# Turning three more normalised chunks with VectorE instead of TensorE, and multiplying token tiles 5 to 8 in a row

## The chip, the cores and the metric

The kernel runs on one core of one Trainium2 chip. A core has five engines that matter here: TensorE (PE, matrix products), VectorE (DVE, elementwise work, reductions and transposes of 32 x 32 blocks), ScalarE (ACT, activations, that is a function of scale times input plus bias), GpSimd (POOL, slower elementwise work) and SyncE (SP, which issues the DMAs between DRAM and the on-chip memory). Each engine works through its own queue in order; semaphores make one engine wait for another. The metric is the time of one execution on the device in microseconds. All times below are microseconds unless marked otherwise.

## What is computed

One block of a transformer over 2048 tokens of width 512: an adaptive layer norm, linear attention with 32 heads, a second adaptive layer norm, and a bilinear feed-forward part.

```python
h = layernorm(x) * (1 + ca) + sa
q, k, v = split_heads(h @ wqkv)
pq, pk = phi(q), phi(k)                  # phi(t) = where(t > 0, t + 1, exp(t)) + 1e-6
kv = einsum("bhsd,bhse->bhde", pk, v);  z = pk.sum(over tokens)
o = (pq @ kv) / (pq . z + 1e-6)
x = x + ga * (o @ wo)
h = layernorm(x) * (1 + cb) + sb
x = x + gb * (((h @ w_gate) * (h @ w_up)) @ w_down)
```

The six vectors sa, ca, ga, sb, cb, gb come from `silu(c) @ w_mod`. Everything is in 32-bit floating point.

## The kernel before, in words

The tokens are cut into four chunks of 512 and each chunk into four token tiles of 128, 16 tiles in all, numbered 0 to 15; tiles 4 to 7 belong to the second chunk. (The change's title counts the tiles 4 to 7 as the fifth to the eighth.) A tile has its 128 tokens on the 128 partitions and 512 features along them. To keep 32-bit accuracy at the faster matmul format, every operand is split into a rounded part and a difference (`split`, L193: a copy with rounding on ScalarE, then a subtraction, mostly on VectorE), and every product is three matmuls: high by high, high by low, low by high (`product`, L207 to L209; 12 matmuls for a projection over four blocks of 128 features).

A projection needs the normalised tokens with features on the partitions, so each chunk is turned once per layer norm. Before the change, `Norm.transpose` (L289) does that for one block of 128 features with four TensorE transposes of 128 x 128 against an identity matrix (L293) into a PSUM bank; `Norm.modulated` (L302) then applies scale and shift on ScalarE and splits.

The order of the work is written out by hand: all queues run in the order of the program text. The pool `tiles` has 94 buffers of 128 x 512; a new tile takes a free buffer.

The main loop (L525) runs over the 16 tiles as steps i = 0 to 15, with i = 4 * chunk + j. In step i TensorE does the key projection of tile i + 2 (`proj`, L325), in steps 3, 4, 6 and 7 also a query projection (`q_at`), then `t_tile(i)` (L368), twelve matmuls that add keys times inputs to four accumulators. ScalarE and VectorE split tile i + 1's inputs and keys (`k_split_x`, `k_split`), apply phi to the projection (`k_phi`), and add up z. In steps j = 2 and 3 they take the statistics of the chunk after the next; in step j = 3 they normalise its first two tiles (`xhat`, L269), in the following step the other two. In the following steps j = 0 and j = 1 (`turn_at`) the chunk is turned, two blocks of features per step, between two halves of `t_tile`. The chunk turned in steps 4 and 5 is first wanted by the key projection in step 6, the one turned in steps 8 and 9 in step 10. `extra` hangs other work on single steps: splits of the value and output weights, parts of the six modulation vectors, loads.

After the loop come the attention's small product, the query tiles and the tail. There the query tiles of the later chunks are already turned by VectorE by a detour: `ready` (L744) divides by the denominator and stores a tile to DRAM with one DMA (`move_out`, L719), `move_in` (L725) reads it back with four DMAs in an order in which transposes of 32 x 32 blocks turn the whole tile, `turn_v` (L733) turns it, `turn_h` and `turn_l` split it. `y_step` (L777) multiplies a turned tile with the output weights (twelve matmuls, L766), starts the next tile's accumulator and takes the statistics of the last one for the second layer norm (`y_b`, L768, `stats_act`, L245). The third and fourth chunk's second norm is also turned by a detour (`stow`, `unstow`, `flip`, `flipped`): ScalarE normalises in an order of blocks (`xhat_blocks`, L275), VectorE turns tile by tile into one wide buffer, ScalarE makes from it one block of 128 features at a time. The first two chunks' second norm is turned by TensorE (`ln2_turn`, L914). `gate_up` (L842, 24 matmuls) and `down` (L865) are the feed-forward part for three of its eleven blocks of columns; the other eight are done by a fast matrix scheme for two chunks together (from L1030 in the profile).

SP issues all DMAs in the order of the program. A DMA that waits, for a free buffer or for data, holds up all those behind it.

## Time and profile before

| | us |
|---|---|
| median of three runs | 554.49 (553.96 to 555.14) |
| the profiled execution | 554.37 |
| span of its instructions | 552.7 |
| TensorE busy | 547.0 |
| VectorE busy | 373.6 |
| ScalarE busy | 291.7 |
| GpSimd busy | 203.4 |

The span runs from the first to the last instruction of the profiled execution; the rest of its time lies around it. Rows of groups give the line, engine, operation, output and input tiles, shapes and count, then the busy sum in microseconds and the mean of one in nanoseconds, then idle time of the engine just before them. Rows of a timeline give the start and the duration in microseconds from the span's start; neighbouring instructions of one line are merged with a count. Matmuls are pipelined: one of 128 x 512 is shown with about 390 ns but the next starts about 227 ns later, so TensorE's pace is read from starts.

### The profile page before, as it was taken

To read this page: it belongs to the slowest core of one execution; us is meant where nothing else is said; L and a number is where in the kernel's file an instruction comes from. 1 tells how busy PE (TensorE), PEld (TensorE's weight loads), DVE (VectorE), ACT (ScalarE), POOL (GpSimd) and SP (SyncE) were. 2 spreads that over 40 slices of the span, in tenths; PEclk is the share of its full clock that TensorE was granted. 3 is DMA by queue.
4 is the path that set the end of the run, shared out by engine and by line. 5 is a ranking of instruction groups with operands and counts; after the bars stand their busy time and mean duration, and the time that the engine had idled before them with its cause. 6 is when DMAs were issued, how large, how long until landed. Compare 5 with 4: busy or idle time off the path is not lost.

```text
span 552.7 us, 7324 instructions
## 1 busy us (share of the span) xinstructions
PE 547.0 (99%) x2488; PEld 449.2 (81%) x2488; DVE 373.6 (68%) x610; ACT 291.7 (53%) x539; POOL 203.4 (37%) x204
## 2 busy tenths in 40 slices
PE   8999999999999999999999999999999999999997
PEld 7788888888888878878888888877888888888886
DVE  7896968986887886778776576985444444434434
ACT  3695856646476667566684545454443444444110
POOL 2000000102003201057596666766666546446200
PEclk9999999999999999999999999999999999999999
DMA  8900203320503205845545071690434222200004
GB/s 284 387 15 2 76 20 103 108 77 1 157 2 133 96 5 186 267 145 135 160 111 155 0 230 38 216 322 2 133 116 132 59 57 59 58 20 0 1 0 152
DMA packets 58373, 58.28 MB, mean 105 GB/s; under 512 B 7328, under 2 KB 38304, under 8 KB 58336
## 3 DMA queue, kind: packets, MB, share of 16 engines
q1 hardware_dynamic: 58336, 57.83, 33.2%
q8 instruction: 19, 0.31, 0.2%
q14 instruction: 18, 0.15, 0.1%
HBM read 42.60 MB, written 15.20 MB: 105 GB/s over the span
## 4 chain that ended last, share of the span: by engine, by line
PE 99%; DVE 0%; issue 0%
PE bank L1030 33%; PE acc L766 7%; PE acc L1110 6%; PE acc L1111 6%; PE acc L1112 6%; PE bank L207 5%; PE bank L209 5%; PE bank L208 5%; PE acc L375 3%; PE acc L374 3%; PE acc L373 3%; PE bank L849 2%; PE bank L851 2%; PE bank L850 2%; PE acc L146 2%; PE bank L293 2%
## 5 line engine op out<-in xcount | busy, mean ns | idle before, releaser
L1030 PE MATMUL bank<-h,w 128*128 128x512 f32 (+1 forms) x798 | 184.7, 390 | 0.0
L1030 PEld LDWEIGHTS bank<-h,w 128*128 128x128 f32 (+1 forms) x798 | 148.4, 186 | 33.4 <-ACT bank L1035 0.7
L1035 ACT ACTIVATE bank<-bank 128x512 f32<-128x512 f32 (+1 forms) x38 | 22.2, 583 | 139.6 <-PE bank L1030 139.5
L836 DVE TENSOR_TENSOR x<-acc,x 128x512 f32<-128x512 f32 (+1 forms) x73 | 48.8, 682 | 48.4 <-PE acc L1112 47.7
L1016 POOL TENSOR_TENSOR w<-raw,w 128x256 fp32r<-128x256 f32 (+3 forms) x38 | 40.9, 1077 | 91.0 <-ACT w L1009 91.0
L1111 PE MATMUL acc<-w,kh 128*128 128x512 f32 (+2 forms) x154 | 59.6, 387 | 0.0
L1110 PE MATMUL acc<-w,kh 128*128 128x512 f32 (+2 forms) x154 | 59.6, 387 | 0.0
L1112 PE MATMUL acc<-w,kl 128*128 128x512 f32 (+2 forms) x154 | 59.5, 386 | 0.0
L263 POOL TENSOR_TENSOR rstd<-ve,half 128x4 f32<-128x4 f32 (+1 forms) x10 | 11.0, 1103 | 121.8 <-DVE ve L262 69.6
L195 POOL TENSOR_TENSOR w<-raw,w 128x512 fp32r<-128x512 f32 (+1 forms) x25 | 35.1, 1409 | 52.2 <-ACT w L194 47.3
L1016 POOL TENSOR_TENSOR w<-t,w 128x512 fp32r<-128x512 f32 (+1 forms) x38 | 49.2, 1318 | 0.0
L195 DVE TENSOR_TENSOR kl<-u,kh 128x512 fp32r<-128x512 f32 (+1 forms) x38 | 26.4, 736 | 30.6 <-ACT kh L194 30.6
L207 PE MATMUL bank<-w,h 128*128 128x512 f32 x104 | 40.9, 394 | 0.0
L209 PE MATMUL bank<-w,h 128*128 128x512 f32 x104 | 40.6, 391 | 0.0
L208 PE MATMUL bank<-w,h 128*128 128x512 f32 x104 | 40.6, 390 | 0.0
L766 PE MATMUL acc<-w,xh 128*128 128x512 f32 x120 | 37.4, 393 | 0.0
L1089 DVE TENSOR_TENSOR u<-bank,u 128x512 f32<-128x512 f32 (+1 forms) x19 | 13.1, 691 | 31.6 <-PE bank L1030 25.1
L1110 PEld LDWEIGHTS acc<-w,kh 128*128 128x128 f32 (+1 forms) x154 | 28.9, 188 | 6.0
L1112 PEld LDWEIGHTS acc<-w,kl 128*128 128x128 f32 (+1 forms) x154 | 28.9, 188 | 5.9
L1111 PEld LDWEIGHTS acc<-w,kh 128*128 128x128 f32 (+1 forms) x154 | 28.9, 188 | 5.9
L998 POOL TENSOR_TENSOR t<-raw,t 128x256 f32<-128x256 f32 (+1 forms) x34 | 25.9, 761 | 1.4
L766 PEld LDWEIGHTS acc<-w,xh 128*128 128x128 f32 x120 | 22.2, 188 | 4.6
(211 smaller groups left out, 1116.5 us busy)
## 6 DMA issues: line engine op xcount, KB each, us to landing
raw<-in_w_mod_dram SPq DMA_DIRECT2D x24, 256.0 KB, 3.7
raw<-in_B_w_down_dram SPq DMA_DIRECT2D x20, 256.0 KB, 3.2
raw<-in_B_w_gate_dram SPq DMA_DIRECT2D x36, 128.0 KB, 3.4
raw<-in_B_w_up_dram SPq DMA_DIRECT2D x36, 128.0 KB, 3.4
x<-in_A_x_dram SPq DMA_DIRECT2D x16, 256.0 KB, 5.4
out_dram<-x SPq DMA_DIRECT2D x15, 256.0 KB, 2.6
raw<-in_A_wqkv_dram SPq DMA_DIRECT2D x12, 256.0 KB, 5.4
moved<-h SPq DMA_DIRECT2D x12, 256.0 KB, 2.1
```

The lines of the kernel that those rows point to most:

```text
L195: (low or nc.vector).tensor_tensor(l, src, f32(h), op=ALU.subtract)
L207: nc.tensor.matmul(ps, ah, bh, start=i == 0, stop=False)
L208: nc.tensor.matmul(ps, ah, bl, start=False, stop=False)
L209: nc.tensor.matmul(ps, al, bh, start=False, stop=i == n - 1)
L766: nc.tensor.matmul(yps[i], x, y, start=False, stop=k == KD - 1 and x is al, skip_group_check=True)
L836: nc.vector.tensor_tensor(xt[:, a:b], dn[j][:, a:b], xt[:, a:b], op=ALU.add)
L998: sub = lambda out, x, y: (on or nc.gpsimd).tensor_tensor(out, x, y, op=ALU.subtract)
L1016: sub = lambda out, x, y: (on or nc.gpsimd).tensor_tensor(out, x, f32(y), op=ALU.subtract)
L1030: mm = lambda x, y, **kw: nc.tensor.matmul(ps, x[:, k], y, skip_group_check=True, **kw)
L1110: nc.tensor.matmul(ps, hh[:, a:b], dh[:n, c:d], start=i == 0, stop=False)
L1111: nc.tensor.matmul(ps, hh[:, a:b], dl[:n, c:d], start=False, stop=False)
L1112: nc.tensor.matmul(ps, hl[:, a:b], dh[:n, c:d], start=False, stop=i == len(hs) - 1)
```

## The change

Three chunks are no longer turned by TensorE: the first layer norm of the third and fourth chunks, and the second layer norm of the second chunk. Each takes the detour by DRAM instead: `xhat_blocks` for four tiles, one store per tile (`lift_out`), four loads per tile (`lift_in`), one VectorE transpose per tile into the wide buffer (`lift_turn`), then per block of 128 features one ScalarE pass with scale and shift (`lift_row`) and the split (`lift_parts`). All four tiles must be turned before the first block can be made. In the loop, all four tiles are normalised and stored at the end of step j = 3, loaded in the following j = 0, and turned and split in j = 1. In step 6 the query projection is put ahead of the key projection; the splits of the output weights move from steps 12 and 13 to 14 and 15. In the tail the query tiles 4 to 7 are multiplied one after the other, ahead of the third `gate_up` and of `down`; tiles 8 to 10 follow `down`; and the denominators, the moves of tiles 8 to 11 and the statistics are put in a new order around them. The first norm's own copies for the third and fourth chunks are now in block order, so `k_split_x` reads them with `by_row`.

```diff
+    LIFTED = (2, 3)
+    def lift_out(name, x):
+        to = tc.dram_tile([P, D], F32, name=name)
+        nc.sync.dma_start(to, x)
+        return to
+    def lift_in(of):
+        v = of.rearrange("(m i) (q c) -> q i m c", i=BL, c=P)
+        u = B("u")
+        for q in range(NQ):
+            nc.sync.dma_start(u[q * BL:(q + 1) * BL].rearrange("i (m c) -> i m c", c=P), v[q])
+        return u
+    def lift_turn(j, u):
+        nc.vector.transpose(wide[:, j].rearrange("p (m s i) -> p m s i", m=NQ, i=BL),
+                            u.rearrange("p (m s i) -> p m s i", m=NQ, i=BL))
+    def lift_row(k, scale, shift):
+        f = B("f")
+        nc.scalar.activation(f.rearrange("p (x i) -> p x i", i=BL),
+                             wide.rearrange("p j (m s i) -> p (j m) s i", m=NQ, i=BL)[:, :, k],
+                             AF.Identity, scale=scale[:, k:k + 1], bias=shift[:, k:k + 1])
+        return f
+    def lift_parts(k, f, cast=True):
+        h, l = B("h", dt=F32R), B("h", dt=F32R)
+        if k % 2 and cast:
+            nc.vector.tensor_copy(h, f)
+        else:
+            nc.scalar.activation(h, f, AF.Copy)
+        nc.vector.tensor_tensor(l, f, f32(h), op=ALU.subtract)
+        return h, l
...
-             12: lambda: (mod_part(4, 2, 3), wo_s.extend(split_raw(x) for x in raw_o[:2]), cols.update({3: col_out(3, mod_col(accs[3], bank()), 0.0)}), mod_load(5)),
...
+             14: lambda: (mod_part(5, 3), wo_s.extend(split_raw(x) for x in raw_o[:2])),
+             15: lambda: wo_s.extend(split_raw(x) for x in raw_o[2:])}
...
-    turn_at = {4 * ch + j: (ch + 1, 2 * j, 2 * j + 1) for ch in range(1, NCH - 1) for j in range(2)}
-    turn_at.update({1: (1, 0, 1), 2: (1, 2, 3)})
+    turn_at = {1: (1, 0, 1), 2: (1, 2, 3)}
...
+        up = ch + 1 if 0 < ch < NCH - 1 else None
+        if i == 6:
+            qps = proj(q_at[i], wq)
         if i > 2:
             ahead[i + 2] = proj(i + 2, wk) if i + 2 < NT else proj(i + 6 - NT, wq)
-        if i in q_at:
+        if i in q_at and i != 6:
             qps = proj(q_at[i], wq)
+        if up and j == 0:
+            lifts = [lift_in(x) for x in lifts]
+        if up and j == 1:
+            lift_turn(0, lifts[0])
...
             k_split(i + 1)
+        if up and j == 1:
+            lift_turn(1, lifts[1])
...
-            nx.xhat(0, 1)
+            nx.xhat_blocks(0, 1)
...
+        if ch + 2 < NCH and j == 3:
+            nx.xhat_blocks(2, 3)
+            lifts = [lift_out(f"first_{ch}_{n}", x) for n, x in enumerate(nx.n)]
...
         t_tile(i, *range(done, KD))
+        if up and j == 1:
+            lift_turn(2, lifts[2])
+            lift_turn(3, lifts[3])
+            for k in range(KD):
+                nx.t[k] = lift_parts(k, lift_row(k, ca, sa), cast=up == 2)
+            norm[up:] = [nx]
...
+    den_a(2, 0, 1, on=nc.vector)
     ln2_turn(0, 0, 1, cast=nc.vector)
...
-    den_a(2, 0, on=nc.vector)
+    turn_h(5)
+    turn_l(5)
+    y_seed(5)
     split_down(f1, nc.gpsimd)
     g()
-    y_step(4, lambda: scale_down(f2), lambda: den_a(2, 1, on=nc.vector))
+    y_step(4, lambda: turn_v(7), lambda: den_a(2, 2, on=nc.vector))
+    y_step(5, lambda: scale_down(f2))
+    y_step(6, lambda: den_a(2, 3, on=nc.vector))
+    y_step(7, turn=False, seed=False)
+    den_b(2)
     g = gate_up(0, f2)
...
+    ready(8, 9)
+    norm2[1].rstd_of(0, 3)
+    y_b(7)
+    ready(10)
+    norm2[1].nmr_of(0, 3)
+    norm2[1].rstd_of(3, 4)
+    norm2[1].xhat_blocks(0, 1, 2)
+    move_in(8, 9)
+    lifts = [lift_out(f"second_1_{n}", norm2[1].n[n]) for n in range(3)]
+    ready(11)
+    norm2[1].nmr_of(3, 4)
+    norm2[1].xhat_blocks(3)
+    lifts.append(lift_out("second_1_3", norm2[1].n[3]))
+    lifts[0], lifts[1] = lift_in(lifts[0]), lift_in(lifts[1])
+    move_in(10)
+    lifts[2], lifts[3] = lift_in(lifts[2]), lift_in(lifts[3])
+    move_in(11)
+    split_down(f2, nc.gpsimd)
     g()
...
+    turn_v(8)
+    turn_h(8)
+    turn_l(8)
+    turn_v(9)
+    turn_h(9)
+    turn_l(9)
+    lift_turn(0, lifts[0])
+    lift_turn(1, lifts[1])
+    take = down(0, parts=((f0, f1), (f2,)), ahead={6: (lambda: y_seed(8, bank),)})
     take()
-    ln2_turn(1, 0, 1)
-    y_step(8, lambda: turn_v(10))
-    ln2_turn(1, 2, 3)
-    y_step(9, lambda: turn_v(11))
+    turn_v(10)
+    y_step(8)
+    lift_turn(2, lifts[2])
+    y_step(9)
+    lift_turn(3, lifts[3])
+    fs = [lift_row(0, cb, sb)]
+    y_step(10)
+    for k in range(KD):
+        if k:
+            fs.append(lift_row(k, cb, sb))
+        nc.sync.dma_start(kept[1][k], fs[k])
+        norm2[1].t[k] = lift_parts(k, fs[k])
+    turn_v(11)
...
     g = gate_up(1, f0)
+    turn_h(11)
     den_a(3, 0, 1, on=nc.vector)
     g()
-    y_step(10)
+    turn_l(11)
```

More of the change, by code (lines that the diff above doesn't have):

```diff
@@ L345, in k_split_x @@
         kx[i] = [B("xh", dt=F32R), B("xl", dt=F32R)]
-        split(norm[ch].n[j], *kx[i])
+        if ch not in LIFTED:
+            split(norm[ch].n[j], *kx[i])
+            return
+        x = by_row(norm[ch].n[j])
+        h, l = (t.rearrange("p (s q i) -> p s q i", q=NQ, i=BL) for t in kx[i])
+        nc.scalar.activation(h, x, AF.Copy)
+        nc.vector.tensor_tensor(l, x, f32(h), op=ALU.subtract)
     def k_phi(i, ps):
@@ L536, in turn_x @@
             norm[to:] = [nx]
-        fresh = i > 0 and ch + 1 < NCH and j == 0
         if i == 2:
@@ L721, in move_out @@
         for i in tiles:
-            moved[i] = tc.dram_tile([P, D], F32, name=f"moved_{i}")
-            nc.sync.dma_start(moved[i], phq.pop(i))
+            moved[i] = lift_out(f"moved_{i}", phq.pop(i))
     def move_in(*tiles):
         for i in tiles:
-            v = moved[i].rearrange("(m i) (q c) -> q i m c", i=BL, c=P)
-            moved[i] = B("u")
-            for q in range(NQ):
-                nc.sync.dma_start(moved[i][q * BL:(q + 1) * BL].rearrange("i (m c) -> i m c", c=P), v[q])
+            moved[i] = lift_in(moved[i])
     def turn_v(i):
@@ L900, in flip @@
         for j in js:
-            nc.vector.transpose(wide[:, j].rearrange("p (m s i) -> p m s i", m=NQ, i=BL),
-                                blocks.pop((ch, j)).rearrange("p (m s i) -> p m s i", m=NQ, i=BL))
+            lift_turn(j, blocks.pop((ch, j)))
     def flipped(ch, *ks):
         for k in ks:
-            f = B("f")
-            nc.scalar.activation(f.rearrange("p (x i) -> p x i", i=BL),
-                                 wide.rearrange("p j (m s i) -> p (j m) s i", m=NQ, i=BL)[:, :, k],
-                                 AF.Identity, scale=cb[:, k:k + 1], bias=sb[:, k:k + 1])
-            blocks[ch, "f", k] = f
+            blocks[ch, "f", k] = lift_row(k, cb, sb)
     stowed, blocks = {}, {}
```

24 lines of the change are left out of this document (2 added, 22 removed).

## The prediction

> **What bounds the kernel now.** I read the page's busy shares and chain first, then what TensorE waited for.
>
> ```profile
> span 552.7 us, 7324 instructions
> PE 547.0 (99%) x2488; PEld 449.2 (81%) x2488; DVE 373.6 (68%) x610; ACT 291.7 (53%) x539; POOL 203.4 (37%) x204
> ...
> PE 99%; DVE 0%; issue 0%
> ```
>
> ```profile
> PE acc L146 <- DVE w L141: 2.0, 1, 2.0
> ```
>
> TensorE is the bound, and its own waits hold one entry, the start. So each microsecond of work taken from TensorE is a microsecond gained, and each microsecond in which it must wait is a microsecond lost: before, there is no slack that could swallow a wait. The question is whether the detour by DRAM, which takes the place of the transposes, is ready when TensorE wants its tiles.
>
> **What is removed.** TensorE in steps 4 to 6 of the main loop, matmuls of one kind per block (L207 starts a projection, L373 the key-times-input product):
>
> ```profile
> 54.41 0.39 PE L373 MATMUL acc<-kh,xh 128*128 128x512 f32 x1
> ...
> 55.79 1.03 PE L293 MATMUL bank<-ident,n 128*128 128x128 f32 x8
> ...
> 58.05 0.39 PE L207 MATMUL bank<-w,h 128*128 128x512 f32 x1
> ...
> 60.77 0.39 PE L373 MATMUL acc<-kh,xh 128*128 128x512 f32 x1
> ...
> 67.11 0.40 PE L207 MATMUL bank<-w,h 128*128 128x512 f32 x1
> ...
> 69.91 0.39 PE L373 MATMUL acc<-kh,xh 128*128 128x512 f32 x1
> ```
>
> Six product matmuls take 55.79 - 54.41 = 1.38, twelve 2.76. From 55.79 to 58.05 stand eight transposes and six such matmuls: 2.26 - 1.38 = 0.88 for eight transposes. A key projection takes 60.77 - 58.05 = 2.72, a query projection 69.91 - 67.11 = 2.80. The change removes six such groups, 48 transposes: **-5.28**.
>
> **What comes in their place**, all from forms that the kernel runs elsewhere; with the transposes' own row, from the groups by line and shape:
>
> ```profile
> L316 DVE TENSOR_TENSOR h<-f,h 128x512 fp32r<-128x512 f32 x23 | 15.9, 692 | 2.1 <-ACT h L315 1.4
> ...
> L293 PE MATMUL bank<-ident,n 128*128 128x128 f32 x80 | 10.4, 272 | 0.0
> ...
> L313 DVE CAST h<-f 128x512 fp32r<-128x512 f32 x19 | 8.5, 449 | 5.5 <-ACT f L305 5.5
> ...
> L907 ACT ACTIVATE f<-wide,col,col 128x512 f32<-128x512 f32 x8 | 6.4, 806 | 0.0
> ...
> L279 ACT ACTIVATE n<-x,nmr,rstd 128x512 f32<-128x512 f32 x8 | 6.2, 804 | 0.0
> ...
> L901 DVE STREAM_TRANSPOSE wide<-u 128x512 f32<-128x512 f32 x8 | 5.5, 699 | 0.0
> ...
> L194 ACT ACTIVATE h<-f 128x512 fp32r<-128x512 f32 x6 | 3.6, 624 | 0.0
> ```
>
> The page's DMA issues (KB each, us to landing), and the landing of the loads' line alone:
>
> ```profile
> u<-moved SPq DMA_DIRECT2D x48, 64.0 KB, 2.0
> moved<-h SPq DMA_DIRECT2D x12, 256.0 KB, 2.1
> ```
>
> ```profile
> DMA to landing us min/median/max: 1.8/2.0/2.7
> ```
>
> SP's timeline, in three stretches:
>
> ```profile
> 25.08 0.33 SPq L113 DMA_DIRECT2D x<-in_A_x_dram  x1
> 61.66 3.02 SPq L113 DMA_DIRECT2D raw<-in_w_mod_dram  x4
> ...
> 206.27 0.94 SPq L723 DMA_DIRECT2D moved<-h  x2
> 208.37 1.75 SPq L731 DMA_DIRECT2D u<-moved  x4
> ...
> 242.71 5.86 SPq L731 DMA_DIRECT2D u<-moved  x12
> ```
>
> Normalising in block order costs what the plain form costs (0.80). Per chunk SP issues 4 stores and 16 loads of 64 KB. Twelve such loads in a row take 5.86, so 0.49 each, and one lands 2.0 after its issue (1.8 to 2.7). In the loop, SP's queue is empty when the first detour comes (25.08 to 61.66); loads that now stand behind the detours (modulation and output weights) wait at most those 8 us and are read a step or more later: 0.
>
> **Third chunk (wanted at step 6).** ScalarE's timeline, step 3 into step 4:
>
> ```profile
> 50.15 1.52 ACT L272 ACTIVATE n<-x,nmr,rstd 128x512 f32<-128x512 f32 x2 [4.27 <-DVE nmr L267]
> ...
> 53.87 0.80 ACT L272 ACTIVATE n<-x,nmr,rstd 128x512 f32<-128x512 f32 x1
> ```
>
> The first two tiles are normalised at 50.15 in both kernels, the third at 53.87; the fourth follows at once, 1.52 - 0.80 = 0.72 later, and ends at 55.39. Its store is issued there. The sixteen loads stand behind all four stores: the last issue is at 55.39 + 0.47 + 15 x 0.49 = 63.2, landing 65.2. Only then can VectorE turn tile four (0.70, 65.9), and only when all four are turned can ScalarE make the first row of 128 features (0.81, 66.7) and its rounded part (0.62, 67.35).
> TensorE without the transposes: 54.41 + 2.76 = 57.17 (step 4), + 2.72 + 2.76 = 62.65 (step 5), + 2.80 for the query projection now put first in step 6 = 65.45. There tile 8 wants the rounded part: idle 1.9. The other three rows then come at the pace of VectorE: difference 0.69, cast 0.45, difference 0.69, difference 0.69, and the last row's cast and difference; ScalarE, with neighbours overlapping by 0.09 (two of 0.80 took 1.52), starts rows 0.72 and casts 0.53 apart, so row four, behind three rows and two casts, ends at 65.9 + 3 x 0.72 + 2 x 0.53 + 0.81 = 69.95. The last cast and difference end at 71.1, and tile 8 ends at 71.4 where 65.45 + 2.72 = 68.2 was possible: **+3.2**. Bounds: 2.2 if the loads are 0.44 apart (1.75 for four) and the last lands in 1.8, 4.0 if it takes 2.7.
>
> **Fourth chunk (wanted at step 10).** No query projection covers it, and its chain starts later, since VectorE's queue was held by the third chunk's parts:
>
> ```profile
> 67.53 0.68 DVE L195 TENSOR_TENSOR xl<-n,xh 128x512 fp32r<-128x512 f32 x1
> ...
> 71.40 0.69 DVE L341 SCALAR_TENSOR_TENSOR h<-bank,h 128x512 f32<-128x512 f32 x1 [0.38 <-ACT h L338]
> ...
> 77.53 0.16 DVE L267 SCALAR_TENSOR_TENSOR nmr<-mv,rstd 128x4 f32<-128x4 f32 x1 [1.21 <-POOL rstd L263]
> ```
>
> ```profile
> 77.73 1.52 ACT L272 ACTIVATE n<-x,nmr,rstd 128x512 f32<-128x512 f32 x2 [4.71 <-DVE nmr L267]
> ```
>
> ```profile
> 78.19 0.39 PE L373 MATMUL acc<-kh,xh 128*128 128x512 f32 x1
> ```
>
> Between 67.53 and 77.53 VectorE works through one list, the same in both kernels, idle 0.38 and, at the end, 1.21 for GpSimd. In the changed kernel it starts when the third chunk's last difference (71.2 with the hand-over) and one weight difference (0.6) are out, at 71.8: 4.3 later. With the 0.38 gone the scale is known at 81.4, normalising starts at 81.6. As in the third chunk the fourth tile ends 5.24 later (86.85), the last load lands 9.8 after that (96.65), turn 97.35, row 98.15, rounded part 98.8.
> TensorE: from 71.4 the product (2.76), step 7's two projections (2.72, 2.80) and product (2.76) end at 82.44; steps 8 and 9 take 5.48 each: 93.4. Idle 5.4. Here all four casts are ScalarE's (cast=False), so a row with its cast takes 0.72 + 0.53 = 1.25: last part 102.45, difference 103.15, tile 12 ends at 103.4 where 96.1 was possible: **+7.3**. Bounds: if VectorE's queue were not late at all, the chain of 103.4 - 81.6 = 21.8 would run against 0.46 + 2.76 + 5.48 + 5.48 + 2.72 = 16.9 of TensorE's work, counted from where TensorE stood at 77.73 (0.46 before step 7's product): +4.9. Above: +8.5, with slow landings, or with a slow clock after the idle time (below). I take 7.3, since VectorE has only 0.38 idle in the list in which it could catch up.
>
> **Second chunk's second norm.** Tiles 4 to 7 now run in a row, so the chain starts 5.5 (24 matmuls) earlier, ahead of 24 + 36 + 36 = 96 matmuls, eight times 2.74 = 21.9.
>
> ```profile
> 207.11 0.60 ACT L250 ACTIVATE x<-acc 128x512 f32<-128x512 f32 x1 [1.22 <-PE acc L766]
> ...
> 208.41 0.19 ACT L251 ACTIVATION_READ_ACCUMULATOR acc<-acc,sums 128x1 f32 x1
> ```
>
> SP is the long part. From about 1.0 after tile 7 (the first load follows its store by 2.1) it issues 8 loads of tiles 8 and 9, three stores, two more stores, 8 lifted loads, 4 for tile 10, 8 lifted: 33 x 0.49 = 16.2, last landing at 18.7. Turn 0.70, row 0.81, then tile 9's statistics (207.11 to 208.60 for one tile, 1.49) stand ahead of the rounded part on ScalarE, then 0.62 and 0.69: 23.0 for the first difference, wanted by gate's second matmul at 22.1: **+0.9**, bounds 0 and 3 (SP's queue late by four more DMAs, 2). Behind VectorE's wait for the first lifted loads stand the evacuation of the feed-forward part and tile 10's turn: tile 10's loads land at 1.0 + 24 x 0.49 + 2.0 = 14.8, it is wanted after 84 matmuls, at 19.2: 0. The rows' stores to DRAM move behind this, read back only for the left sides: 0. Tiles 5 to 7 in a row want, each 2.74 of TensorE, a turn, a difference and a denominator's two passes of some 0.7 (estimate by L316), 2.8: even, 0, bounds 0 and 0.6. Denominators moved ahead of the first chunk's turn fall into an idle time:
>
> ```profile
> 177.39 0.95 DVE L313 CAST h<-f 128x512 fp32r<-128x512 f32 x1 [3.54 <-ACT f L305]
> ```
>
> Two of them take four passes, some 2.8, there: 0. Without that gap they would cost up to 2.8.
>
> **Output-weight splits moved to steps 14 and 15.**
>
> ```profile
> 132.33 1.89 DVE L195 TENSOR_TENSOR w<-n,w 128x512 fp32r<-128x512 f32 x3
> ```
>
> ```profile
> 134.59 0.22 PE L207 MATMUL bank<-w,w 128*128 128x128 f32 x1
> ```
>
> The last difference ends at 134.2; its matmul is the eleventh from 134.59 at 0.11 apart, 135.7. Slack 1.5 against two differences (1.2) and ScalarE's two casts ahead (1.0): **+0.2**, bounds 0 and 0.7.
>
> **Sum**: -5.28 + 3.2 + 7.3 + 0.9 + 0.2 = +6.3 on the profiled execution's 554.37 (0.12 under the median 554.49): 560.7. Bounds: -5.28 + 2.2 + 4.9 = +1.8, 556.2; -5.28 + 4.0 + 8.5 + 3 + 0.6 + 0.7 = +11.5, 565.9.
>
> **Rivals.** (A) Faster, by one mechanism: loads issued closer together. If SP issued the sixteen loads at the 0.33 of one DMA alone (25.08 row) and not 0.49, each detour shortens by 2.4; the third chunk's wait falls to 0.8, and with it VectorE's lateness, so the fourth's to about 4.9 - 2.4 = 2.5. The second norm's becomes 0: -5.28 + 0.8 + 2.5 + 0.2 = -1.8, 552.6. It decides below 0.37 per load. Against it: 5.86 for twelve.
> (B) The clock slows in the fourth chunk's 5.4 idle.
>
> ```profile
> 2.00:5.00 3.00, 3.00 (x7) 2.42 (x8) 1.11 (x3) 0.08 (x1) 0.60 (x5) 1.00 0.75 237
> 5.00:10.00 5.00, 5.00 (x18) 3.97 (x18) 3.91 (x15) 0.92 (x2) 1.67 (x2) 1.00 0.99 332
> ```
>
> After the start's idle time the first 7 matmuls took 3.00, 0.43 each, against 0.23 later, though the granted-clock column says 1.00; 25 took 8.00 where 25 x 0.227 = 5.7: 2.3 lost. After 98.8, tile 12's matmuls wait for parts anyway (three in 1.25, which 3 x 0.43 just fills), so most is hidden: +0.4, or the full +2.3 if the slow stretch begins only with the dense matmuls: 563.0. The Trainium skill ("TensorE: Matmul & The Clock Gate", Part 1, what is happening) says that the array's clock is halved after about one idle window of 3.4 us and released after as much activity; the start agrees, and no row of this kernel shows it after a pause. By that rule the third chunk's 1.9 costs nothing and the fourth's 5.4 may.
> (C) SP's queue at the second norm runs later: +3 there instead of +0.9, 562.8.
> (D) The waits are real but VectorE catches up: third 2.2, fourth 4.9: 557.3 with the other terms kept.
>
> **Numbers.** Forecast with its neighbours D, C: 0.60, 0.10, 0.07; B in full 0.10; A 0.13, of which 0.03 ends within 0.2% (1.1 us, about what a measurement of this kernel can tell from no change). The likeliest one's own range is 557 to 563. The range 555.5 to 564.5 leaves A out and little above. Faster 0.10, same 0.03, slower 0.87.
>
> **What would show it.** In the changed kernel's waits of TensorE: two large entries, tile 8's projection waiting some 2 us and tile 12's some 5 us at once, for ScalarE's rounded part, then smaller ones for differences; the chain of waits leading there through the vector transposes to the loads on SP, sixteen in about 7.8. L293 at x32, and its time down from 10.4 by 6/10. TensorE's busy time down by about 5.3 and its idle time up by about 11. Gate of chunk two starting with a wait under 1.5. I am wrong if TensorE shows no wait at tile 12, if the loads are issued faster than 0.4 apart, or if the scale of the fourth chunk is known before step 7's projections end.

## The result, and the profile after

| | before | changed |
|---|---|---|
| median of five runs, us | 554.75 (553.96 to 555.72) | 567.86 (567.34 to 568.37) |
| ratio | | 1.0235, 95% interval 1.022 to 1.025 |
| the profiled execution, us | 554.37 | 568.37 |

Slower, as forecast, by 13.1 us where 6.3 was forecast; 567.86 lies above the range of 555.5 to 564.5. The top of the changed kernel's page, and what its TensorE waited for:

```profile
span 566.6 us, 7360 instructions
PE 549.7 (97%) x2440; PEld 446.2 (79%) x2440; DVE 381.9 (67%) x619; ACT 294.5 (52%) x543; POOL 204.7 (36%) x206
...
PE 82%; ACT 5%; DVE 4%; SPq 3%; DMA 2%; issue 2%; DVEq 0%; ACTq 0%
```

```profile
PE bank L207 <- ACT h L351: 6.5, 2, 4.9
PE acc L146 <- DVE w L141: 2.0, 1, 2.0
PE bank L898 <- ACT h L351: 1.5, 1, 1.5
PE acc L815 <- DVE xl L762: 1.2, 1, 1.2
PE acc L926 <- DVE kl L195: 0.7, 1, 0.7
PE acc L815 <- ACT acc L806: 0.6, 1, 0.6
```

Before, the second of these lines was alone. TensorE's idle time is now 566.6 - 549.7 = 16.9 where it was 5.7, and the chain that ended last leaves TensorE for 18% of the span where it was 1%. To see where the 14 us came in, I compare the starts of the same matmuls in the two traces (of the last one, its end):

| us | before | changed | lost in the stretch before it |
|---|---|---|---|
| first projection of step 3 (L207) | 37.89 | 39.23 | 1.34: start |
| row sum behind the loop (L183) | 139.90 | 149.37 | 8.13: loop |
| first matmul of gate (L849, now L898) | 179.46 | 188.88 | -0.05 |
| first of the long matmul row of the tail (L1030, now L1074) | 260.79 | 274.70 | 4.49: tail |
| last matmul, its end | 549.07 | 563.03 | 0.05 |

**The loop's two waits.** TensorE at tile 8 and at tile 12:

```profile
66.52 0.40 PE L209 MATMUL bank<-w,h 128*128 128x512 f32 x1
68.49 0.50 PE L207 MATMUL bank<-w,h 128*128 128x512 f32 x1 [1.58 <-ACT h L351]
...
72.87 0.39 PE L414 MATMUL acc<-kh,xh 128*128 128x512 f32 x1
```

```profile
94.56 0.39 PE L416 MATMUL acc<-kl,xh 128*128 128x512 f32 x1
99.82 0.80 PE L207 MATMUL bank<-w,h 128*128 128x512 f32 x1 [4.87 <-ACT h L351]
...
105.37 0.44 PE L414 MATMUL acc<-kh,xh 128*128 128x512 f32 x1
```

Tile 8 could have begun at 66.75 and ended 2.72 later, at 69.47; it ended at 72.87, a loss of 3.40. Tile 12 could have ended at 94.79 + 2.72 = 97.51 and ended at 105.37: 7.86. The queue that fed tile 8, on SP and then on VectorE:

```profile
52.35 4.73 SPq L324 DMA_DIRECT2D first<-n  x4
57.18 7.53 SPq L332 DMA_DIRECT2D u<-first  x16
```

```profile
61.40 0.69 DVE L195 TENSOR_TENSOR w<-raw,w 128x512 fp32r<-128x512 f32 x1
62.00 0.70 DVE L336 STREAM_TRANSPOSE wide<-u 128x512 f32<-128x512 f32 x1
62.63 0.65 DVE L195 TENSOR_TENSOR xl<-n,xh 128x512 fp32r<-128x512 f32 x1
63.20 0.68 DVE L406 SCALAR_TENSOR_TENSOR kl<-phi,kh 128x512 fp32r<-128x512 f32 x1
63.80 0.71 DVE L336 STREAM_TRANSPOSE wide<-u 128x512 f32<-128x512 f32 x1
...
65.59 1.34 DVE L336 STREAM_TRANSPOSE wide<-u 128x512 f32<-128x512 f32 x2
```

The sixteen loads take 7.53 and the fourth turn ends at 66.93, so far as the prediction had it. But read VectorE's list: it has no gap from 61.40 on, and four passes of other work stand between the turns. By the profile's chain the last load landed at 66.20, and the list reaches the fourth turn at the same moment. So the loads and this list end together; which one binds the trace alone does not say (e6 and e9 below).

**The clock.** Stretches of the changed kernel around tile 12 (length, busy time and instructions of TensorE, its weight loads, VectorE, ScalarE and GpSimd, then the granted clock):

```profile
95.22:98.63 3.41, 0.00 (x0) 0.00 (x0) 2.97 (x5) 0.33 (x1) 0.00 (x0) 1.00 0.70 193
98.63:102.05 3.42, 2.23 (x5) 1.42 (x6) 1.38 (x2) 3.33 (x6) 0.00 (x0) 0.50 0.94 307
102.05:105.46 3.41, 3.41 (x9) 2.15 (x9) 2.21 (x4) 2.92 (x5) 0.00 (x0) 0.50 0.50 190
```

After the empty stretch the clock is 0.50 for 6.83, and matmuls start 0.43 apart. The record shows the same for 3.41 at 16.7 in the start, in code that did not change: 24 matmuls fall between 15 and 21 where there were 30 before, and six at 0.227 are the table's 1.34.

**The tail.** TensorE, ScalarE and VectorE where it lost time:

```profile
227.04 0.39 PE L815 MATMUL bank<-w,xl 128*128 128x512 f32 x1
228.05 0.73 PE L815 MATMUL acc<-w,xh 128*128 128x512 f32 x2 [0.62 <-ACT acc L806]
...
233.64 0.39 PE L815 MATMUL acc<-w,xl 128*128 128x512 f32 x1
235.52 0.50 PE L898 MATMUL bank<-h,w 128*128 128x512 f32 x1 [1.49 <-ACT h L351]
236.25 0.50 PE L899 MATMUL bank<-h,w 128*128 128x512 f32 x1 [0.22 <-DVE h L352]
```

```profile
262.52 0.50 PE L926 MATMUL acc<-w,kl 96*128 96x512 f32 x1 [0.67 <-DVE kl L195]
...
265.47 0.50 PE L815 MATMUL acc<-w,xl 128*128 128x512 f32 x1 [1.16 <-DVE xl L762]
```

```profile
226.07 0.71 DVE L336 STREAM_TRANSPOSE wide<-u 128x512 f32<-128x512 f32 x1 [2.77 <-DMA u<-second]
226.71 2.44 DVE L885 TENSOR_TENSOR x<-acc,x 128x512 f32<-128x512 f32 x4
...
261.17 1.30 DVE L195 TENSOR_TENSOR kl<-phi,kh 96x512 fp32r<-96x512 f32 x1
263.56 1.86 DVE L762 TENSOR_TENSOR xl<-f,xh 128x512 fp32r<-128x512 f32 x1 [1.09 <-ACT xh L758]
```

Three places. Tile 9 starts 1.01 after the matmul before it instead of 0.23: a loss of 0.8, because VectorE stood 2.77 at the second lifted tile, whose loads had not landed (the profile gives this line's landings as 1.8 to 3.7), and the evacuation that seeds tile 9's accumulator was queued behind. Gate starts 1.65 late, and its second matmul 0.5 more. And 25 us later, where the prediction had nothing, the second chunk's feed-forward part waits 0.3 + 0.8 + 1.3 for the parts that ScalarE and VectorE hand it. Together some 5.4 of the 6.25 that this tail's waits must have cost, since 16 transposes went (1.76) and it still lost 4.49.

The lateness of the third place is handed on: the profile's chain goes back from the matmul at 265.47 through passes of VectorE and ScalarE alone to the lifted parts, and from there to the loads that SP issued. But 1.2 of its 2.5 is the length of one pass. The pass at 263.56 took 1.86; the same pass in the kernel before:

```profile
249.50 0.69 DVE L709 TENSOR_TENSOR xl<-f,xh 128x512 fp32r<-128x512 f32 x1 [1.08 <-ACT xh L705]
```

GpSimd works beside it in both (the last section has what the traces show of that). The pass at 261.17 took 1.30, but 1.25 before too, where TensorE did not have to wait for it.

### The profile page after: what moved, and what is told of

Its sections match the earlier page's. It is cut to its first block, busy times and chain, and to the rows that moved or that the text cites. A ratio compares the mean times of both kernels' runs of the same rounds, so it can differ in the third digit from the quotient of the medians.

```text
span 566.6 us, 7360 instructions
## 1 busy us (share of the span) xinstructions
PE 549.7 (97%) x2440; PEld 446.2 (79%) x2440; DVE 381.9 (67%) x619; ACT 294.5 (52%) x543; POOL 204.7 (36%) x206
## 4 chain that ended last, share of the span: by engine, by line
PE 82%; ACT 5%; DVE 4%; SPq 3%; DMA 2%; issue 2%; DVEq 0%; ACTq 0%
PE bank L1074 32%; PE acc L1155 6%; PE acc L1154 6%; PE acc L1156 6%; PE acc L815 5%; PE bank L207 4%; PE bank L209 4%; PE bank L208 4%; SPq L332 2%; PE acc L416 2%; PE acc L415 2%; PE acc L414 2%; DMA raw<-in_w_mod_dram 1%; ACT n L279 1%; ACT f L341 1%
## 5 line engine op out<-in xcount | busy, mean ns | idle before, releaser
L1074 PE MATMUL bank<-h,w 128*128 128x512 f32 (+1 forms) x798 | 184.7, 390 | 0.0
L1074 PEld LDWEIGHTS bank<-h,w 128*128 128x128 f32 (+1 forms) x798 | 148.5, 186 | 33.2 <-ACT bank L1079 0.7
L263 POOL TENSOR_TENSOR rstd<-ve,half 128x4 f32<-128x4 f32 (+3 forms) x11 | 11.8, 1072 | 126.0 <-DVE ve L262 74.0
L195 POOL TENSOR_TENSOR w<-raw,w 128x512 fp32r<-128x512 f32 (+1 forms) x26 | 36.4, 1403 | 56.0 <-ACT w L194 51.5
L207 PE MATMUL bank<-w,h 128*128 128x512 f32 x104 | 42.7, 411 | 6.5 <-ACT h L351 6.5
L209 PE MATMUL bank<-w,h 128*128 128x512 f32 x104 | 42.1, 405 | 0.1
L208 PE MATMUL bank<-w,h 128*128 128x512 f32 x104 | 41.6, 400 | 0.0
L1133 DVE TENSOR_TENSOR u<-bank,u 128x512 f32<-128x512 f32 (+1 forms) x19 | 13.1, 691 | 31.4 <-PE bank L1074 24.9
L207 PEld LDWEIGHTS bank<-w,h 128*128 128x128 f32 x104 | 20.0, 192 | 12.6 <-ACT h L351 8.4
```

The costliest lines, as they stand in the source:

```text
L195: (low or nc.vector).tensor_tensor(l, src, f32(h), op=ALU.subtract)
L207: nc.tensor.matmul(ps, ah, bh, start=i == 0, stop=False)
L208: nc.tensor.matmul(ps, ah, bl, start=False, stop=False)
L209: nc.tensor.matmul(ps, al, bh, start=False, stop=i == n - 1)
L1074: mm = lambda x, y, **kw: nc.tensor.matmul(ps, x[:, k], y, skip_group_check=True, **kw)
```

## The experiments

Times of each group are beside runs of the kernel before on the same chip (554.46, 554.63, 554.92 and 554.45 us for e1 to e4, e5 to e8, e9 to e11, and e12). The table splits each profile as above; every execution has its own start, so the stretches say more than the sum. In all of them the two stretches left out are within 0.5 of before.

| run | median us (range) | ratio to before, 95% | start | loop | tail |
|---|---|---|---|---|---|
| changed | 567.86 (567.34 to 568.37) | 1.022 to 1.025 | 1.34 | 8.13 | 4.49 |
| e1 loop undone | 560.54 (558.93 to 562.6) | 1.0079 to 1.0139 | 0.96 | 0.39 | 3.38 |
| e2 tail undone | 563.31 (562.8 to 565.16) | 1.0142 to 1.0185 | 0.20 | 8.11 | -0.03 |
| e3 third chunk only | 563.0 (561.71 to 564.17) | 1.0123 to 1.0165 | 0.16 | 3.12 | 6.35 |
| e4 fourth chunk only | 564.05 (563.77 to 567.15) | 1.0154 to 1.0212 | 3.19 | 4.86 | 4.54 |
| e5 idle matmuls | 566.32 (565.31 to 567.43) | 1.0184 to 1.023 | 0.02 | 7.49 | 3.49 |
| e6 four tiles together | 567.59 (565.13 to 568.6) | 1.0195 to 1.0251 | 0.21 | 7.67 | 6.29 |
| e7 tail's order | 567.8 (566.92 to 568.5) | 1.0215 to 1.0249 | 0.20 | 8.37 | 4.74 |
| e8 denominators on GpSimd | 566.45 (565.25 to 567.43) | 1.0196 to 1.0233 | 0.02 | 7.90 | 2.90 |
| e9 e6 and turns in a row | 564.35 (563.57 to 565.6) | 1.0152 to 1.0191 | 1.55 | 4.18 | 4.30 |
| e10 begun sooner, tail undone | 555.9 (554.8 to 558.41) | 1.0006 to 1.0032 | 1.06 | 1.41 | 0.92 |
| e11 loads by GpSimd | 569.85 (567.5 to 570.5) | 1.024 to 1.0281 | -0.27 | 8.10 | 7.58 |
| e12 sooner still | 553.15 (552.07 to 554.52) | 0.9964 to 0.9983 | 0.81 | -2.11 | -0.01 |

### Which part loses what: e1 to e4

```diff
# e1
-    LIFTED = (2, 3)
+    LIFTED = ()
# e2: from move_in(5) to gate of the second chunk, the text of the kernel before
# e3
+    LIFTED = (2,)
# e4
+    LIFTED = (3,)
```

With a chunk left out of `LIFTED`, its norm is turned by TensorE in the order of the kernel before.

> The first norm of the third and fourth chunks goes back to TensorE; the second chunk's second norm and the tail stay as changed. My theory: the losses are local and add up. In the changed kernel's trace the loop as a whole loses some 7.7 us against before, the output weights' splits 0.4, the tail up to the second gate 1.5 and the waits at the second down product 3.0. So this kernel should take about 554.75 + 0.4 + 1.5 + 3.0 = 559.7 us (558.7 to 560.7), with TensorE's waits in the loop gone and those in the tail unchanged. Rival: the tail's waits are handed on from VectorE's and SP's lateness in the loop; then they go too, and the time is that of before less eight plus eight transposes, about 553 to 555.

> The tail is that of before (second norm of the second chunk turned by TensorE, tiles 4 to 7 in their old places); the loop keeps both detours. Losses local: 554.75 + 7.7 + 0.4 = 562.9 us (562 to 564), waits at tile 8 (about 2 us) and tile 12 (about 5 us) as in the changed kernel, none in the tail. Rival, losses handed on: about the changed kernel's time less only what the tail's own TensorE work differs by, 566 to 568.

> Only the third chunk's first norm takes the detour in the loop, the fourth goes back to TensorE; tail as changed. The third chunk's own balance is 3.2 lost to waits less 1.76 saved, +1.4; with the tail's 4.9: 554.75 + 1.4 + 4.9 = 561.1 us (560 to 562). If the fourth chunk's loss stays without its detour (VectorE late from the third chunk), 564 or more.

> Only the fourth chunk's first norm takes the detour, the third goes back to TensorE; tail as changed. My theory says that the fourth chunk's wait is partly handed on: VectorE entered its list 4.3 us late because of the third chunk's parts. Without that the wait should fall from about 5.3 idle to about 3, too short for the halved clock, and tile 12's loss from 7.9 to about 4.9: 554.75 + 4.9 - 1.76 + 4.9 = 562.8 us. Rival: the fourth chunk's wait is its own (its chain of stores, loads, turns and rows is just longer than the two steps it has): loss 7 to 8, idle above 5, 565 to 566 us.

e1 and e2 come out inside their ranges. The losses are local in the main: the loop loses 8.11 without the new tail, and the tail 3.38 without the loop's detours. e1's loop still loses 0.39, the moved splits.

e3 misses: 563.0, where 560 to 562 was expected and 564 or more for the rival. Its granted clock was 0.50 for 3.41 from 68.58, behind tile 8's wait, so tile 8 lost 4.2 and not 3.40; and it was 0.50 for 6.83 from 229.00, behind gate's wait, which is some 2.5 of its tail's 6.35. As it ran, e3 puts the third chunk at 3.12 - 0.39 = +2.7.

e4 lies between its two expectations. The wait at tile 12 fell to 3.1 as expected, but the clock was halved behind it all the same (0.50 for 6.83 from 97.33). The fourth chunk costs 4.86 - 0.39 = +4.5 alone, and with the 16 transposes that it saves (1.76) its wait costs 6.2, where 4.9 was expected. In the changed kernel it cost 7.86, so 1.6 was inherited from the third chunk, through VectorE's queue: beside the start, the fourth chunk's scale was known 3.6 later there than in e4. The prediction had put the inheritance at 7.3 - 4.9 = 2.4.

### The clock's share: e5

```diff
-    def proj(i, w, of=bank):
+    def proj(i, w, of=bank, fill=0):
...
+        for _ in range(fill):
+            nc.tensor.matmul(ps, idle[:, :P], idle, start=True, stop=True)
...
-            ahead[i + 2] = proj(i + 2, wk) if i + 2 < NT else ...
+            ahead[i + 2] = proj(i + 2, wk, fill={6: 6, 10: 22}.get(i, 0)) if i + 2 < NT else ...
```

> The changed kernel, with 6 idle matmuls of 128x128 ahead of tile 8's projection and 22 ahead of tile 12's, so that TensorE does something during part of both waits; their results are never read. It asks what part of the loop's +8.1 is the slower clock (98.6 to 105.5 at half in the changed kernel's record). Theory 1, the waits for the parts are the loss and the clock adds little, since tile 12's matmuls wait for their parts anyway: loop +7.5 to +8.1, time 567 to 568. Theory 2, the clock is a term of its own: no half clock near 98 to 105, tile 12's projection ends at about 104.1 rather than 105.4, loop +6.8, time 566.5. In both the parts come as late as before, so nothing below 566.

The stretch of tile 12, in which the granted clock is now 1.00:

```profile
98.60:103.50 4.90, 4.47 (x13) 1.77 (x12) 2.87 (x5) 4.79 (x8) 0.00 (x0) 1.00 0.75 262
```

Tile 12 ended at 103.47, from a start 1.32 earlier: 0.6 sooner. So the clock took 0.6 in the loop. The loop's 7.49 is the lower end of the first expectation, the time, 566.32, is near the second's; rival B's own price was 0.4 to 2.3. Its mechanism was real and its price small, because tile 12's matmuls wait for parts anyway. The median fell by 1.5; the other 0.9 isn't settled (this execution had neither the start's slow stretch nor tile 9's wait).

### Loads or VectorE's list: e6 and e9

```diff
# e6
-            nx.xhat_blocks(0, 1)
+            nx.xhat_blocks(0, 1, 2, 3)
+            lifts = [lift_out(f"first_{ch}_{n}", x) for n, x in enumerate(nx.n)]
...
-        if ch + 2 < NCH and j == 3:
-            nx.xhat_blocks(2, 3)
-            lifts = [lift_out(f"first_{ch}_{n}", x) for n, x in enumerate(nx.n)]
# e9, on top of e6
         if up and j == 1:
-            lift_turn(0, lifts[0])
+            for n in range(NJ):
+                lift_turn(n, lifts[n])
...
-            lift_turn(1, lifts[1])
...
-            lift_turn(2, lifts[2])
-            lift_turn(3, lifts[3])
```

> The changed kernel, with all four tiles of the next chunk normalised and stored together, ahead of the key features and the query of the step, rather than two and two around them. It moves the fourth store, behind which all sixteen loads stand, about 2.3 earlier in both chunks. Theory 1, the loads' landing sets both waits: tile 8's idle 2.0 goes to 0 and the third chunk costs 1 rather than 3.1, VectorE hands on 2 less, tile 12's idle 5.3 becomes 1 to 2: loop +8.1 becomes +2 to +3.5, time 562 to 563.5. Theory 2, ScalarE is needed for the key features too: they come 1.5 later and TensorE waits for them instead at steps 4 and 8, loop +5 to +7, time 565 to 567.

> The kernel of e6 (all four tiles normalised and stored together), with VectorE's four turns of the lifted tiles in one row ahead of the splits, the key features and the running sum of their step, rather than one, one and two between them. In e6 the loads were issued 2.3 earlier beside the start and the first row of features came no earlier. Theory 1, VectorE's list was as tight as the loads: six passes of 0.68 stood between the first turn and the last, so now that both are moved tile 8's idle of 1.9 goes (loop +7.7 becomes +4 to +5.5 with what tile 12 inherits), time 564 to 565.5. Theory 2, something else (ScalarE, or a landing) sets the first row: loop stays at +7.5 to +8, time 567 to 568.

SP and VectorE in e6, and VectorE in e9:

```profile
53.74 7.53 SPq L332 DMA_DIRECT2D u<-first  x16
```

```profile
60.86 0.70 DVE L336 STREAM_TRANSPOSE wide<-u 128x512 f32<-128x512 f32 x1
...
64.45 1.29 DVE L336 STREAM_TRANSPOSE wide<-u 128x512 f32<-128x512 f32 x2
```

```profile
62.20 1.89 DVE L336 STREAM_TRANSPOSE wide<-u 128x512 f32<-128x512 f32 x3
64.31 0.71 DVE L336 STREAM_TRANSPOSE wide<-u 128x512 f32<-128x512 f32 x1 [0.21 <-DMA u<-first]
```

e6 misses both its expectations. The loads began 57.18 - 53.74 = 3.4 earlier (2.3 beside the start), the last turn ended only 1.2 earlier, of which the start's difference is 1.1: tile 8 waited as long as before. VectorE's list was as tight as the loads. With the turns also taken out of that list (e9) the loop falls from 7.67 to 4.18, inside e9's expectation. The earlier loads alone pay next to nothing (8.13 to 7.67); both together are worth some 4 us. The turns in a row alone were not run; with the last landing at 66.20, as in the changed kernel, the fourth turn could not have ended before 66.9, where it ended anyway.

### The tail: e7, e8 and e11

```diff
# e7
-    lift_turn(1, lifts[1])
     take = down(0, ...)
     take()
+    lift_turn(1, lifts[1])
...
-    fs = [lift_row(0, cb, sb)]
-    y_step(10)
+    fs = []
     for k in range(KD):
-        if k:
-            fs.append(lift_row(k, cb, sb))
+        if k == 1:
+            y_step(10)
+        fs.append(lift_row(k, cb, sb))
# e8
-    den_a(3, 0, 1, on=nc.vector)
+    den_a(3, 0, 1)
...
-    den_a(3, 2, 3, on=nc.vector)
+    den_a(3, 2, 3)
# e11: lift_in issues on the queue it is given
-    lifts[0], lifts[1] = lift_in(lifts[0]), lift_in(lifts[1])
+    split_down(f2, nc.gpsimd)
+    lifts = [lift_in(x, nc.gpsimd) for x in lifts]
     move_in(10)
-    lifts[2], lifts[3] = lift_in(lifts[2]), lift_in(lifts[3])
     move_in(11)
-    split_down(f2, nc.gpsimd)
```

> The changed kernel, with the turn of the second lifted tile moved behind the evacuation of the second chunk's feed-forward part, and the first row's parts put ahead of tile 10's statistics. Theory 1, the tail's first loss is order alone (VectorE stands at a turn whose loads are not there, 223.3 to 226.1; ScalarE does tile 9's statistics ahead of the rounded part): tile 9's wait of 1.0 and gate's waits of 1.9 and 0.7 shrink to 1.5 in all, tail +4.5 becomes +2 to +2.5, time 565.5 to 566. Theory 2, the loads' landing sets gate's start whatever the order: tail +4 to +4.5, time 567.3 to 568.

> The changed kernel, with the products of the denominators of tiles 12 to 15 done by GpSimd rather than VectorE, between gate of the second chunk and its second part. Theory 1, the 3 us that TensorE loses between 260.6 and 265.8 are VectorE's queue, which ran 3 late from the lifted parts on: four passes of 0.7 less on VectorE there, those waits fall to 0 to 1, tail +4.5 becomes +1.5 to +2.5, time 565 to 566. Theory 2, ScalarE's chain (the scale of the third chunk's second norm) sets them, and VectorE's queue is not what it waits for: tail unchanged, time 567.5 to 568.5; or worse, if GpSimd slows VectorE's passes.

> The changed kernel, with the sixteen lifted loads of the second norm issued by GpSimd rather than by SP, where they stood among twenty others; the last down weights' split is put ahead of them. Theory 1 (rival C of the prediction: SP's queue is what is late at the second norm), the last lifted tile can be turned at about 224 rather than 229, gate's waits of 2.0 and 0.7 shrink to under 1, VectorE hands on 2 less and the second loss shrinks too: tail +4.5 becomes 0 to +2, time 563.5 to 565.5. Theory 2, ScalarE and VectorE's orders set gate's start, or GpSimd issues no faster: tail +3.4 to +4.5, time 566.5 to 568.

e7 goes by its second theory: tile 9's wait went, a loss of 0.6 inside tile 10 and a later second row of gate took its place, and the tail stayed at 4.74. These two moves buy nothing there.

e8 cuts the second loss nearly in half, and misses its first expectation narrowly (566.45 against 565 to 566, tail 2.90 against 2.5 at most). Its waits in the place of the 0.7 and 1.2 above:

```profile
PE acc L815 <- DVE xl L762: 0.5, 1, 0.5
PE acc L815 <- ACT xh L758: 0.5, 1, 0.5
```

From start to start of the matmuls the second loss is 0.6 + 0.7 = 1.3, where e5, with the same tail as the changed kernel, has 0.3 + 0.8 + 1.3 = 2.4. So four passes of some 0.7 fewer on VectorE take away 1.1 of it. Not all of that need be the queue: the pass that ends the loss took 1.24 in e8 and 1.84 in e5, beside GpSimd's passes in both, and that difference of 0.6 is a matter of how the two engines' passes fall together. What is left, in which ScalarE is late too, stays open. The tail as a whole is only 0.6 shorter than e5's, since gate started 0.3 later in this execution and small gaps take the rest.

e11 is worse than either of its expectations. GpSimd's issues, and VectorE behind them:

```profile
217.30 7.25 POOL L332 DMA_DIRECT2D u<-second  x13 [1.66 <-DMA second<-n]
```

```profile
225.98 0.71 DVE L336 STREAM_TRANSPOSE wide<-u 128x512 f32<-128x512 f32 x1 [2.92 <-DMA u<-second]
```

Thirteen issues in 7.25 are 0.56 each against SP's 0.47, and landings reach 4.9. The second turn came no earlier (225.98 against 226.07, and beside the start 1.5 later), tile 9 waited 2.3, and the clock halved twice in this tail (at 227.88 and 265.43). So GpSimd's queue, whose issues are no faster, does not help. Whether SP's queue alone sets gate's start, which is rival C, e11 does not settle: it put a slower queue in SP's place.

### Lead time, or the work itself: e10 and e12

```diff
# e10 (tail of the kernel before)
         if i == 2:
             nx2 = Norm(xts[2])
             nx2.stats(0, 1)
         if i == 3:
             nx2.stats(2, 3); nx2.rstd_of()
             nx3 = Norm(xts[3]); nx3.stats(0, 1, 2, 3); nx3.rstd_of()
             nx2.xhat_blocks(0, 1, 2, 3)
             lifts = [lift_out(...) for ... in nx2.n]
         if i == 4: lifts = [lift_in(x) for x in lifts]; nx3.nmr_of()
         if i == 5: lift_turn 0 to 3, ahead of the splits; rows and parts behind them
         if i == 6:
             nx3.xhat_blocks(0, 1, 2, 3)
             lifts = [lift_out(...) for ... in nx3.n]
         if i == 7: lifts = [lift_in(x) for x in lifts]
         if i == 8: lift_turn 0 to 3, at the end
         if i == 9: rows and parts, behind the splits
# e12, on top of e10
         if i == 2: nx2.stats(0, 1, 2, 3); nx2.rstd_of()
         if i == 3: nx2.nmr_of(); nx2.xhat_blocks(0, 1), ahead of the splits
         if i == 6: lift_in right behind lift_out
         wo_s back in extra[12] and extra[13]
```

This diff is abridged: it lists the steps' new content in the code's names.

> All of the layer norms' detours in the loop begun where VectorE and ScalarE stand idle: both chunks' statistics in step 3, the third chunk normalised there in one go, its loads in step 4, its four turns in a row at the head of step 5; the fourth chunk normalised and stored at the end of step 6, loaded in step 7, turned at the end of step 8, its rows made in step 9. The tail is that of the kernel before, and the output weights' splits stay moved. Theory 1, the loss in the loop is lead time alone (the chain started too late, and behind VectorE's list): both waits go, what is left is -5.28 + 0.39 of the splits and up to 2 of the rows' pace, loop -5 to -3, time 549.5 to 551.5, faster than before. Theory 2, the detour's own work on VectorE (eight turns of 0.70) and ScalarE (eight rows of 0.81) costs it wherever it stands, since TensorE then waits for key features or splits: loop -1 to +3, time 553.5 to 557.5.

> e10 with three edits, each for a wait that its trace still shows. The third chunk's statistics all stand in step 2 and its normalising ahead of the splits of step 3 (in e10 the scale was known at 51.2 and the first row came at 64.6); the fourth chunk's loads stand right behind its stores, ahead of the modulation's weights (in e10 the stores were out at 77.1, the first load at 80.0, the last landing at 90.9, tile 12's first wait at 92.2); the output weights' splits are back in steps 12 and 13, where the kernel before has them. Of the 48 transposes 32 are the loop's, 3.52, and 16 the tail's, 1.76, so the loop can come to -3.5 at best and not to -5. Theory 1, lead time: tile 8's 0.8 and tile 12's 3.5 go and the splits' 0.39 with them, loop +1.4 becomes -3.5 to -2, time 551 to 552.8. Theory 2, the work itself: the waits move to key features and splits, loop 0 to +1.5, time 554.5 to 556.

e10 misses the first expectation, which was set too low: it counted all 48 transposes in the loop, where only 32 are. It lies in the second's ranges (loop 1.41, 555.9), so it does not speak for lead time by itself. (Its tail, that of the kernel before, lost 0.92 in this execution; 0.6 of that is a wait for a VectorE pass that took 1.46 beside GpSimd.) Its trace shows what was left, at SP:

```profile
77.26 2.64 SPq L113 DMA_DIRECT2D raw<-in_w_mod_dram  x4
80.00 8.44 SPq L332 DMA_DIRECT2D u<-first  x16
```

The detour's stores were out at 77.1, and its loads stand behind four loads of modulation weights. With those behind them instead, and the third chunk's chain begun sooner (e12):

```profile
76.05 8.93 SPq L332 DMA_DIRECT2D u<-first  x16
```

```profile
88.31 0.82 ACT L341 ACTIVATE f<-wide,col,col 128x512 f32<-128x512 f32 x1 [2.33 <-DVE wide L336]
```

```profile
PE acc L146 <- DVE w L141: 2.0, 1, 2.0
```

Tile 12's first row is made at 88.31, where the changed kernel had 98.30, and TensorE's list of waits is again the start alone. The loop is at -2.11, inside the first expectation; the time, 553.15, is 0.35 above its range. The same 32 turns, done by the same eight VectorE passes and eight ScalarE rows, now make the kernel faster than before: ratio 0.9973 (0.9964 to 0.9983). So the work fits, against e12's second theory. What cost 8 us was when it began and where its loads and turns stood in the queues; e10 and e12 move these together, and no run beyond e6 and e9 tells them apart.

## Why the prediction was right or wrong

By its own steps, in the changed kernel's profile:

| step | predicted | measured |
|---|---|---|
| 48 transposes removed | -5.28 | taken as it stood; L293 is at x32 |
| third chunk | +3.2 | +3.40; 4.2 in e3 |
| fourth chunk | +7.3 | +7.86, of it 0.6 the clock |
| output-weight splits | +0.2 | +0.39 (e1) |
| second norm of the second chunk, and the tail around it | +0.9 | 4.49 + 1.76 = +6.25; with the same tail from 5.1 (e1) to 8.1 (e3) |
| start | 0 | +1.34 in this execution |

**What held.** The loop: -3.52 + 3.2 + 7.3 + 0.2 = +7.2 against +8.1. TensorE waits at tile 8 and tile 12 for ScalarE's rounded part, the chain runs back to SP, sixteen loads take 7.53 (7.8 predicted), and the fourth chunk inherits its lateness from the third (e4). Rival A would have needed 0.37 for a load; they are 0.47 apart. Rival D asked for a wait of 2.2 and 4.9 in all; they lost 3.40 and 7.86. That the third chunk came out so near its 3.2 is partly luck: behind the same wait the clock stayed at 1.00 in this execution and fell to 0.50 in e3, e6, e7, e8 and e11.

**What failed is the term "Second chunk's second norm", +0.9 with bounds 0 and 3.** The trace shows three errors in it. Gate's start itself, 0.9 predicted, lost 2.1: the last lifted load was issued at 229.1, some 18 after tile 7 instead of 17 (one issue on the way took 1.52), and ScalarE put two tiles' statistics around the first row. "Behind VectorE's wait for the first lifted loads stand the evacuation of the feed-forward part and tile 10's turn ...: 0" priced tile 10 and not the evacuation, whose lateness tile 9 paid with 0.8 (in this execution and in e6; e1, e3, e4 and e5 do not have it). And the term ended where gate starts: VectorE, late with the lifted parts until 239.4, handed its lateness to the second chunk's feed-forward part 25 us on, 2.5 more, of which 1.2 is the one pass that took 1.86 instead of 0.69 beside GpSimd. e8, with four passes fewer on VectorE, loses 1.1 less there. The bounds came from SP's queue alone, so they could not hold the other two.

**A bound that was wrong though its term held.** "2.2 if the loads are 0.44 apart": e6 brought the loads forward by 2.3 and tile 8 gained nothing. The prediction treated the loads as the one chain and VectorE's list as something that fills the time beside it. They were equally long.

**The signs in the trace that it named.** TensorE's idle time up by about 11: 11.2. Its busy time down by 5.3: it rose by 2.7, since matmuls at half clock are counted longer and more of the pieces stand apart, so this sign tells little. Gate's wait under 1.5: 1.49 in the list, but the start is 1.65 late, and it was not the only one. None of the three signs of being wrong came: tile 12 waited, the loads were 0.47 apart, and the fourth chunk's scale was known at 82.7, after step 7's projections had ended at 81.15.

## What to carry to other kernels

A detour that takes an engine off the critical path needs lead time on every queue that it crosses. Before pricing it by its longest transfer, list what else each queue holds between its steps: here the loads and VectorE's list were equally long, and moving the loads alone gave nothing back. Follow an engine's lateness past the first place that waits for it, until a gap in its list swallows it: in the tail that was 25 us further on. And when the same work begun earlier fits, begin it earlier rather than drop it: e12 has the same turns and is faster than the kernel before.

## What the runs showed of the hardware

**The clock halves after a thin stretch, not only after an empty one.** Slow stretches lie on a grid of 3.41 us: in e8 they begin at 68.34 and 99.06, nine times 3.413 apart. Three pairs of neighbouring stretches of that grid, from e6, e11 and the changed kernel, each pair in order of time:

```profile
65.97:69.39 3.42, 2.08 (x6) 0.97 (x7) 1.83 (x4) 3.36 (x6) 0.00 (x0) 1.00 0.21 68
69.39:72.80 3.41, 3.41 (x9) 2.67 (x9) 3.36 (x6) 2.65 (x5) 0.00 (x0) 0.50 0.00 0
```

```profile
262.02:265.43 3.41, 2.36 (x9) 1.08 (x8) 1.74 (x3) 3.41 (x7) 3.41 (x3) 1.00 0.56 152
265.43:268.85 3.42, 3.42 (x9) 2.68 (x10) 3.21 (x7) 2.31 (x5) 3.34 (x4) 0.50 0.56 134
```

```profile
64.50:67.91 3.41, 2.41 (x11) 1.61 (x9) 2.43 (x5) 0.91 (x2) 0.00 (x0) 1.00 0.76 228
67.91:71.33 3.42, 2.84 (x9) 1.35 (x9) 2.58 (x5) 3.39 (x6) 0.00 (x0) 1.00 0.37 135
```

At 0.227 apart fifteen matmuls fit into a stretch. In e6 six fall in one, and the next runs at half speed; in the changed kernel eleven and nine, and the clock stays. The count alone is not the rule, since e11's nine were followed by half speed. Of all such stretches between 40 and 545 us in the fourteen traces, those with six matmuls or fewer were always followed by half clock, those with ten or more never, and of those with seven to nine some were and some were not. So a gap of 1.97 left the clock alone in the changed kernel, where it fell across two stretches, and a gap of 1.93 in e6 halved it. The Trainium skill ("TensorE: Matmul & The Clock Gate", Part 1) describes a free-running window of 3.413 us, which these runs show too. The same part of the Trainium skill gives the rule that idle gaps should not exceed about 3.4 us; these runs show that shorter ones can halve the clock. The prediction had drawn from that rule that a wait of 1.9 costs nothing, which held in the changed kernel and not in e6.

**VectorE's passes stretch while GpSimd works.** The two passes at 261.17 and 263.56 shown above took 1.30 and 1.86 where the same forms take 0.69 elsewhere. Over the fourteen traces, passes of these two forms took at most 0.69 wherever no GpSimd instruction ran beside them (405 passes), and up to 1.86 where one did. GpSimd at that time, in the changed kernel:

```profile
261.87 2.99 POOL L992 TENSOR_TENSOR s<-f,f 128x512 f32<-128x512 f32 x2
```

The Trainium skill ("SBUF — State Buffer", "SBUF: two separate sides") says that a VectorE pass with two operands in this memory and a GpSimd pass that reads it lock each other out for a whole instruction, which agrees; no run here took GpSimd's work away to test it.

**Landings spread.** A load of 64 KB landed 2.0 after its issue by the median, but 3.7 at the longest in the changed kernel and 4.9 in e11. What sets the long ones is open; e5 and the changed kernel have the same tail, and tile 9 waited in one of these two executions only.
